# Transposing k and q of batches 2 to 7 on TensorE instead of by DMA

## The chip, the cores and the metric

The kernel runs on one core of a Trainium2 chip. The metric is the time of one execution in microseconds, as the device counts it. TensorE (PE in the profile), VectorE (DVE), ScalarE (ACT), GpSimd (POOL) and the sync engine (SP, which here only issues DMAs) each work through a list of instructions of their own, in order, and wait for each other by semaphores.

## The reference, cut to what matters

```python
def sm_attn(qq, kk, vv):
    s = scale * np.matmul(qq, kk.transpose(0, 1, 3, 2))
    a = np.exp(s - np.max(s, axis=-1, keepdims=True))
    return np.matmul(a / (np.sum(a, axis=-1, keepdims=True) + 1e-09), vv)

p_packed = sm_attn(p, k, v)              # 8 batches, 8 heads, 32 packed rows of 64
attn = sm_attn(q, p_packed, p_packed)    # 576 rows a head
x = attn.transpose(0, 2, 1, 3).reshape(4608, 512)
h = x @ w_in                             # 512 x 2048
g = h * (1.0 / (1.0 + np.exp(-beta * h)))
out = g @ w_out                          # 2048 x 512
```

## The kernel before

The work goes batch by batch, eight batches of 576 rows. For one batch `b`, in the names that the lists of the kernel use:

- `ld`, `cast`: k, v and q are loaded in float32 by DMAs of SP (L446, L454; L461 for batches 0 and 1) and cast to bfloat16, for batches 2 to 7 on GpSimd (L481, L487).
- `tr`, `trr`, `T`, `rk`, `rq`: k and q are transposed, so that the 64 elements of a head lie on partitions. For batches 0 and 1 (`PE_BATCHES = 2`) TensorE does it (L399): one `tr` is eight 128x128 transposes into one PSUM bank, `trr` the last two; an evacuation of each bank follows on VectorE or ScalarE (`T`, L547 and L549, of 128x1024; `rk` and `rq`, L570 and L572, of 128x256). For batches 2 to 7 one DMA transpose each does it (L559), from SBUF to SBUF, issued by SP.
- `s1`, `e1`, `z1`, `pun`, `pp`: the first attention (scores, exponent, sums, product with v, pack).
- `s2`, `e2`, `z2`, `l2`, `n2`, `A2`: the scores of the second attention, their exponents, and these divided by their sums.
- `w`, `W`: the packed values are multiplied with `w_in` first, so that the second attention and the first layer become one product.
- `h`, `g` (`hr`, `gr` for the last 64 rows): that product, 16 pieces of 128x512, and silu on ScalarE (L944).
- `o` and `take` (`add` for batch 0): the product with `w_out` and its evacuation. In batches 1 to 7 the first 512 rows go by Strassen's scheme: seven products `p`/`P` per batch, with the sums `S` of g on VectorE (L1150), sums of `w_out` once (`T4`, L1124), and the reads `R` of the banks (L1180, L1182).
- `store`: DMAs to the output, issued by SP.

PSUM has eight banks here: 2 for `h`, 2 for `o`, and 4 for everything of attention (`att`), transposes and `w` included.

The order in which each engine does these tasks is written out in `SEQUENCE`, one list for each engine. `Planner.run` walks the lists and emits the instructions in that order. With its own table of costs it also places *fillers*: 128x128 matmuls on a tile of ones (`keep_warm`, into a bank of `o`), where it expects TensorE to be idle in the first 60 us (`WARM_UNTIL`). They are real instructions and take their time, whether TensorE would have been idle or not.

Of the kernel before, what the change touches and what calls it, by code (L numbers as in the profile page):

```python
# [8 lines left out]
B, H, S, D = 8, 8, 576, 64  # L9
# [6 lines left out]
bf16 = mybir.dt.bfloat16  # L16
# [9 lines left out]
TS = 9  # L26
# [17 lines left out]
LAG = 0.4  # L44
# [4 lines left out]
def TILED(key):  # L49
# [14 lines left out]
        ("p0_tr",), ("tr", 0, "k", 0), ("bcol",), ("tr", 0, "k", 1), ("brow", 0), ("trr", 0, "k"), ("s1r", 0),  # L64
        ("s1", 0, 0), ("s1", 0, 1), ("tr", 0, "q", 0), ("brow", 1), ("z1", 0), ("tr", 0, "q", 1), ("trr", 0, "q"),
        ("pun", 0, 0), ("pun", 0), ("tr", 1, "k", 0), ("s2", 0, 0), ("z2", 0, 0), ("tr", 1, "k", 1), ("trr", 1, "k"),
        ("z2", 0, 1), ("brow", 2), ("s2", 0, 1), ("w", 0, 0), ("s1r", 1), ("s1", 1, 1), ("s1", 1, 0), ("z2", 0, 2),
        ("h", 0, 1), ("h", 0, 0), ("w", 0, 1), ("h", 0, 2), ("tr", 1, "q", 0), ("z1", 1), ("h", 0, 3), ("h", 0, 7),
        ("pun", 1, 0), ("h", 0, 4), ("h", 0, 6), ("pun", 1), ("tr", 1, "q", 1), ("h", 0, 5), ("brow", 3),
        ("o", 0, 2, 1), ("o", 0, 3, 1), ("o", 0, 3, 3), ("s2", 1, 0), ("o", 0, 2, 3), ("o", 0, 3, 5), ("o", 0, 2, 5),  # L70
        ("z2", 1, 0), ("o", 0, 2, 7), ("z2", 1, 1), ("o", 0, 3, 7), ("w", 0, 2), ("o", 0, 0, 1), ("o", 0, 0, 3),
        ("o", 0, 0, 5), ("w", 1, 0), ("o", 0, 1, 1), ("o", 0, 1, 3), ("h", 0, 8), ("h", 0, 11), ("w", 0, 3),
        ("w", 1, 1), ("h", 0, 10), ("o", 0, 1, 5), ("o", 0, 0, 7), ("h", 0, 9), ("h", 0, 14), ("w", 1, 2),
        ("h", 0, 13), ("h", 0, 15), ("o", 0, 1, 7), ("trr", 1, "q"), ("p_tr", 0), ("h", 0, 12), ("h", 1, 6),
        ("o", 0, 0, 9), ("h", 1, 1), ("h", 1, 4), ("w", 1, 3), ("o", 0, 1, 9), ("h", 1, 11), ("h", 1, 2), ("p_tr", 1),
        ("o", 0, 0, 11), ("h", 1, 8), ("h", 1, 0), ("o", 0, 0, 13), ("o", 0, 1, 11), ("h", 1, 9), ("o", 0, 0, 15),
        ("h", 1, 12), ("o", 0, 1, 13), ("h", 1, 10), ("o", 0, 1, 15), ("o", 0, 3, 9), ("s2", 1, 1), ("o", 0, 3, 11),
        ("s1r", 2), ("s1", 2, 0), ("o", 0, 3, 13), ("o", 0, 3, 15), ("s1", 2, 1), ("o", 0, 2, 9), ("o", 0, 2, 11),
        ("h", 1, 3), ("o", 0, 2, 13), ("o", 0, 2, 15), ("h", 1, 14), ("z1", 2), ("h", 1, 5), ("p", 1, 1, 0),
        ("z2", 1, 2), ("h", 1, 13), ("h", 1, 7), ("p", 1, 1, 1), ("pun", 2, 0), ("h", 1, 15), ("p", 1, 1, 2),  # L80
        ("pun", 2), ("P", 1, 1), ("p", 1, 2, 0), ("p", 1, 2, 1), ("p", 1, 2, 2), ("s2", 2, 0), ("s2", 2, 1),
        ("hr", 0, 0), ("P", 1, 2), ("hr", 0, 1), ("z2", 2, 0), ("p", 1, 6, 0), ("p", 1, 6, 1), ("p", 1, 6, 2),
        ("P", 1, 6), ("w", 2, 0), ("p", 1, 5, 0), ("p", 1, 5, 1), ("p", 1, 5, 2), ("p", 1, 7, 0), ("s1r", 3),
        ("P", 1, 5), ("s1", 3, 1), ("p", 1, 7, 1), ("z2", 2, 1), ("p", 1, 7, 2), ("P", 1, 7), ("p", 1, 3, 0),
        ("p", 1, 3, 1), ("z2", 2, 2), ("s1", 3, 0), ("hr", 1, 0), ("p", 1, 4, 0), ("p", 1, 4, 1), ("w", 2, 2),
        ("p", 1, 4, 2), ("h", 2, 6), ("P", 1, 4), ("h", 2, 1), ("p", 1, 3, 2), ("h", 2, 2), ("z1", 3), ("h", 2, 8),
        ("o", 1, 4, 1), ("h", 2, 9), ("P", 1, 3), ("h", 2, 11), ("pun", 3, 0), ("pun", 3), ("hr", 1, 1),
        ("o", 1, 4, 3), ("h", 2, 3), ("w", 3, 0), ("h", 2, 12), ("h", 2, 13), ("o", 1, 4, 5), ("o", 1, 4, 7),
        ("h", 2, 7), ("h", 2, 15), ("o", 1, 4, 9), ("o", 1, 4, 11), ("h", 2, 0), ("w", 3, 2), ("h", 2, 14),
        ("h", 2, 4), ("o", 1, 4, 13), ("p", 2, 1, 0), ("h", 2, 5), ("h", 2, 10), ("o", 1, 4, 15), ("p", 2, 1, 1),  # L90
        ("p", 2, 1, 2), ("s2", 3, 0), ("s2", 3, 1), ("P", 2, 1), ("p", 2, 2, 0), ("p", 2, 2, 1), ("p", 2, 2, 2),
        ("z2", 3, 0), ("P", 2, 2), ("z2", 3, 1), ("p", 2, 6, 0), ("p", 2, 6, 1), ("p", 2, 6, 2), ("z2", 3, 2),
        ("P", 2, 6), ("s1r", 4), ("s1", 4, 0), ("p", 2, 5, 0), ("s1", 4, 1), ("p", 2, 5, 1), ("p", 2, 5, 2),
        ("P", 2, 5), ("h", 3, 8), ("z1", 4), ("hr", 2, 0), ("p", 2, 7, 0), ("p", 2, 7, 1), ("h", 3, 12), ("h", 3, 13),
        ("pun", 4, 0), ("pun", 4), ("hr", 2, 1), ("p", 2, 7, 2), ("h", 3, 10), ("P", 2, 7), ("h", 3, 9), ("w", 4, 0),
        ("h", 3, 3), ("h", 3, 1), ("p", 2, 3, 0), ("p", 2, 3, 1), ("h", 3, 2), ("h", 3, 15), ("p", 2, 4, 0),
        ("p", 2, 4, 1), ("h", 3, 11), ("h", 3, 5), ("p", 2, 3, 2), ("p", 2, 4, 2), ("h", 3, 6), ("w", 4, 2),
        ("h", 3, 7), ("h", 3, 0), ("P", 2, 4), ("P", 2, 3), ("h", 3, 4), ("h", 3, 14), ("p", 3, 1, 0), ("p", 3, 1, 1),
        ("p", 3, 1, 2), ("P", 3, 1), ("s2", 4, 0), ("s2", 4, 1), ("p", 3, 2, 0), ("p", 3, 2, 1), ("p", 3, 2, 2),
        ("z2", 4, 0), ("P", 3, 2), ("z2", 4, 1), ("p", 3, 6, 0), ("p", 3, 6, 1), ("p", 3, 6, 2), ("P", 3, 6),  # L100
        ("s1r", 5), ("s1", 5, 1), ("z2", 4, 2), ("s1", 5, 0), ("p", 3, 5, 0), ("p", 3, 5, 1), ("p", 3, 5, 2),
        ("P", 3, 5), ("hr", 3, 0), ("p", 3, 7, 0), ("h", 4, 6), ("p", 3, 7, 1), ("p", 3, 7, 2), ("z1", 5),
        ("h", 4, 13), ("hr", 3, 1), ("P", 3, 7), ("p", 3, 3, 0), ("h", 4, 12), ("h", 4, 1), ("pun", 5, 0), ("pun", 5),
        ("p", 3, 3, 1), ("h", 4, 14), ("h", 4, 15), ("w", 5, 0), ("h", 4, 4), ("p", 3, 4, 0), ("h", 4, 2),
        ("p", 3, 3, 2), ("h", 4, 8), ("p", 3, 4, 1), ("h", 4, 9), ("p", 3, 4, 2), ("h", 4, 0), ("w", 5, 2),
        ("h", 4, 7), ("h", 4, 3), ("P", 3, 4), ("P", 3, 3), ("h", 4, 10), ("h", 4, 5), ("o", 3, 4, 1), ("o", 3, 4, 3),
        ("h", 4, 11), ("p", 4, 1, 0), ("p", 4, 1, 1), ("p", 4, 1, 2), ("s2", 5, 0), ("s2", 5, 1), ("P", 4, 1),
        ("o", 3, 4, 5), ("o", 3, 4, 7), ("z2", 5, 0), ("o", 3, 4, 9), ("o", 3, 4, 11), ("z2", 5, 1), ("z2", 5, 2),
        ("o", 3, 4, 13), ("hr", 4, 0), ("o", 3, 4, 15), ("hr", 4, 1), ("p", 4, 6, 0), ("p", 4, 6, 1), ("p", 4, 6, 2),
        ("p", 4, 2, 0), ("p", 4, 2, 1), ("P", 4, 6), ("h", 5, 1), ("h", 5, 15), ("p", 4, 2, 2), ("s1r", 6),  # L110
        ("s1", 6, 1), ("h", 5, 3), ("h", 5, 10), ("P", 4, 2), ("p", 4, 7, 0), ("s1", 6, 0), ("h", 5, 7),
        ("p", 4, 7, 1), ("p", 4, 5, 0), ("p", 4, 5, 1), ("p", 4, 5, 2), ("P", 4, 5), ("h", 5, 13), ("p", 4, 7, 2),
        ("P", 4, 7), ("z1", 6), ("pun", 6, 0), ("pun", 6), ("h", 5, 4), ("h", 5, 8), ("p", 4, 4, 0), ("p", 4, 4, 1),
        ("h", 5, 6), ("h", 5, 9), ("w", 6, 0), ("h", 5, 11), ("p", 4, 4, 2), ("h", 5, 0), ("P", 4, 4), ("h", 5, 14),
        ("p", 4, 3, 0), ("h", 5, 5), ("p", 4, 3, 1), ("h", 5, 2), ("p", 4, 3, 2), ("h", 5, 12), ("P", 4, 3),
        ("p", 5, 1, 0), ("p", 5, 1, 1), ("p", 5, 1, 2), ("s2", 6, 0), ("s2", 6, 1), ("P", 5, 1), ("p", 5, 2, 0),
        ("p", 5, 2, 1), ("p", 5, 2, 2), ("P", 5, 2), ("p", 5, 6, 0), ("z2", 6, 0), ("z2", 6, 1), ("p", 5, 6, 1),
        ("p", 5, 6, 2), ("P", 5, 6), ("s1r", 7), ("s1", 7, 0), ("z2", 6, 2), ("s1", 7, 1), ("p", 5, 5, 0),
        ("p", 5, 5, 1), ("p", 5, 5, 2), ("hr", 5, 0), ("p", 5, 7, 0), ("P", 5, 5), ("p", 5, 7, 1), ("p", 5, 7, 2),
        ("P", 5, 7), ("w", 6, 2), ("h", 6, 0), ("h", 6, 5), ("p", 5, 3, 0), ("p", 5, 3, 1), ("hr", 5, 1),  # L120
        ("h", 6, 10), ("p", 5, 3, 2), ("p", 5, 4, 0), ("h", 6, 3), ("p", 5, 4, 1), ("h", 6, 9), ("p", 5, 4, 2),
        ("h", 6, 4), ("P", 5, 3), ("h", 6, 15), ("z1", 7), ("h", 6, 1), ("P", 5, 4), ("h", 6, 2), ("pun", 7, 0),
        ("h", 6, 14), ("o", 5, 4, 1), ("pun", 7), ("h", 6, 13), ("o", 5, 4, 3), ("o", 5, 4, 5), ("h", 6, 8),
# [239 lines left out]
class Kernel:  # L363
# [160 lines left out]
    def readers(self, b, x):  # L524

        if b < 0:
            return []
        return [("pun", b)] if x == "v" else [("tr", b, x, 0), ("tr", b, x, 1)] + [("trr", b, x)] * (b < PE_BATCHES)
# [966 lines left out]
```

## Time and profile before

| What | Value |
|---|---|
| time, median of 3 runs | 241.2 us (240.27 to 241.45) |
| the profiled execution | 240.81 us, of which 239.0 us are the span that the profile shows |
| TensorE | 231.6 us busy (97%), 2598 matmuls, granted clock 1.0 throughout |
| weight loads of TensorE | 158.0 us (66%), beside the matmuls |
| VectorE, ScalarE, GpSimd | 155.4 us (65%), 179.3 us (75%), 62.4 us (26%) |
| the DMA queue of SP | its packets took 82.1% of 16 engines' span, 53.62 MB |
| fillers | 196 matmuls on ones |
| DMA transposes | 6 of k, 6 of q |

The busy share of TensorE counts each matmul from start to end, and matmuls overlap: a 128x512 matmul of `h` lasts 380 ns, but the chain of waits shows four of them in a row as 0.86 us, one every 215 ns. So the time that a matmul costs its engine is read from the distance of two starts, and a full bar may hide small gaps.

### The profile page before, as it was taken

What the parts mean: (1) busy time and instruction counts of PE and PEld (TensorE: products, weight loads), DVE (VectorE), ACT (ScalarE), POOL (GpSimd) and SP (SyncE); (2) the same over time, 40 slices, a digit from 0 to 9 for tenths busy, and PEclk for the clock granted to TensorE, in tenths of its full rate; (3) what the DMA queues carried; (4) which work ended last, traced back from release to release, by engine and by line L of the source; (5) the groups of instructions that cost most, each with busy time, mean ns of one, the idle gap of its engine ahead of it and who ended that gap; (6) DMA issues with size and microseconds to landing.
All of it is one profiled execution on the core that took longest, in us unless ns stands there. A gap on an engine that the chain in (4) does not pass through costs nothing.

```text
span 239.0 us, 6151 instructions
## 1 busy us (share of the span) xinstructions
PE 231.6 (97%) x2598; PEld 158.0 (66%) x2598; DVE 155.4 (65%) x249; ACT 179.3 (75%) x318; POOL 62.4 (26%) x75
## 2 busy tenths in 40 slices
PE   7999999999979999999999999999999999999994
PEld 7777643444567754786588656785786647668893
DVE  2646878899669947877495555656668167814731
ACT  4758889889769875996699678796886769768410
POOL 3051305333430660573032604080016000000000
PEclk9999999999999999999999999999999999999999
DMA  6999999999999999998999999949695632003033
GB/s 222 394 387 388 410 367 347 280 313 235 270 215 276 287 229 214 333 272 150 181 306 310 198 272 209 297 100 223 165 319 166 148 129 48 0 0 151 27 132 90
DMA packets 67267, 54.14 MB, mean 227 GB/s; under 512 B 38980, under 2 KB 58820, under 8 KB 66728
## 3 DMA queue, kind: packets, MB, share of 16 engines
q1 hardware_dynamic: 67072, 53.62, 82.1%
q8 instruction: 20, 0.33, 0.6%
q10 hardware_dynamic: 168, 0.14, 0.2%
q14 instruction: 7, 0.06, 0.1%
HBM read 37.23 MB, written 9.44 MB: 195 GB/s over the span
## 4 chain that ended last, share of the span: by engine, by line
PE 74%; DMA 16%; DVE 3%; SPq 3%; issue 1%; POOL 1%; ACT 1%; POOLq 0%
PE o_ps L394 42%; PE h_ps L394 19%; DMA w_out<-in_moe_w_out_dram 9%; DMA qT<-q_bf 3%; PE hr_ps L394 3%; PE w_ps L394 3%; DMA v<-in_v_dram 3%; PE s_ps L394 2%; SPq L559 2%; PE z_ps L394 2%; DMA p<-in_p_dram 2%; PE pp_ps L394 1%; DVE w_out_bf L1413 1%; SPq L461 1%; PE brow_ps L394 1%
## 5 line engine op out<-in xcount | busy, mean ns | idle before, releaser
L944 ACT ACTIVATE g_main<-h_ps 128x512 bf16<-128x512 f32 x128 | 72.3, 596 | 30.0 <-PE h_ps L394 29.4
L394 PEld LDWEIGHTS <-g_main 128*128 128x128 bf16 x624 | 59.0, 98 | 25.6 <-issue 3.2
L394 PE MATMUL h_ps<-A2T,W_bf 128*128 128x512 bf16 x256 | 70.6, 380 | 0.2
L394 PE MATMUL o_ps<-w_out_bf,g_main 128*128 128x256 bf16 (+1 forms) x400 | 61.2, 290 | 0.0
L909 DVE SCALAR_TENSOR_TENSOR W_bf<-w_ps,rz,beta_bc 128x512 bf16<-128x512 f32 x64 | 44.6, 744 | 16.3 <-PE w_ps L394 16.1
L394 PEld LDWEIGHTS <-W_bf 128*128 128x128 bf16 x512 | 32.0, 98 | 19.4 <-issue 5.2
L409 ACT ACT_TABLE_LOAD x24 | 30.8, 1283 | 1.1 <-PEq L1479 0.7
L394 PE MATMUL o_ps<-w_sum,g_main 128*128 128x256 bf16 x224 | 31.0, 273 | 0.0
L481 POOL CAST v_bf<-v 128x1024 bf16<-128x1024 f32 x12 | 14.0, 1182 | 58.9 <-DMA v<-in_v_dram 58.9
L1180 DVE TENSOR_TENSOR o_sb<-o_ps,o_sb 128x512 f32<-128x512 f32 x21 | 14.4, 688 | 21.1 <-PE o_ps L394 14.9
L394 PE MATMUL o_ps<-w_sum,g_sum 128*128 128x256 bf16 x224 | 28.1, 273 | 0.0
L394 PEld LDWEIGHTS <-g_sum 128*128 128x128 bf16 x224 | 21.2, 98 | 3.9 <-issue 0.8
L481 POOL CAST q_bf<-q 128x1024 bf16<-128x1024 f32 x12 | 13.2, 1122 | 21.4 <-DMA q<-in_q_dram 15.9
L394 PE MATMUL o_ps<-ones 128*128 128x128 bf16 x196 | 16.0, 238 | 1.1 <-DVE ones L1245 1.1
L394 PE MATMUL o_ps<-w_out_bf,g_rem 128*128 128x512 bf16 (+1 forms) x80 | 16.8, 337 | 0.0
L394 PEld LDWEIGHTS <-ones 128*128 128x128 bf16 x196 | 13.5, 108 | 3.7 <-issue 2.0
L1182 DVE COPY o_sb<-o_ps 128x512 f32<-128x512 f32 x13 | 8.9, 688 | 8.7 <-PE o_ps L394 8.7
L481 POOL CAST k_bf<-k 128x1024 bf16<-128x1024 f32 x12 | 12.4, 1040 | 8.5 <-DMA k<-in_k_dram 4.8
L850 DVE TENSOR_TENSOR A2T<-E2T,rz 128x512 bf16<-128x512 bf16 x16 | 12.2, 782 | 3.3 <-ACT rz L845 3.3
L964 ACT ACTIVATE g_rem<-hr_ps 128x512 bf16<-128x512 f32 x16 | 9.3, 597 | 4.6 <-PE hr_ps L394 4.5
L809 ACT ACTIVATE E2T<-s_ps,rz 128x512 bf16<-128x512 f32 x16 | 10.5, 686 | 2.7 <-PE s2r_ps L394 2.2
L394 PEld LDWEIGHTS <-g_rem 128*128 128x128 bf16 x80 | 7.6, 98 | 5.0
(114 smaller groups left out, 267.1 us busy)
## 6 DMA issues: line engine op xcount, KB each, us to landing
k<-in_k_dram SPq DMA_DIRECT2D x6, 1024.0 KB, 10.2
q<-in_q_dram SPq DMA_DIRECT2D x6, 1024.0 KB, 9.7
v<-in_v_dram SPq DMA_DIRECT2D x6, 1024.0 KB, 6.4
out_dram<-o_sb SPq DMA_DIRECT2D x10, 512.0 KB, 3.1
w_in<-in_moe_w_in_dram SPq DMA_DIRECT2D x4, 1024.0 KB, 10.7
w_out<-in_moe_w_out_dram SPq DMA_DIRECT2D x4, 1024.0 KB, 11.3
out_dram<-o_sb SPq DMA_DIRECT2D x12, 256.0 KB, 4.3
k<-in_k_dram SPq DMA_DIRECT2D x4, 576.0 KB, 6.3
```

The lines of the kernel that those rows point to most:

```text
L394: return self.nc.tensor.matmul(out, lhsT, rhs, start=start, stop=stop, tile_position=pos, skip_group_check=True)
L409: self.nc.scalar.preload_act_table_set(SETS[mode])
L461: nc.sync.dma_start(t[:].rearrange("p (i e f) -> p i e f", i=2, e=2)[:, i], src[b].rearrange("(e i a) (s t) d -> i (a s) e (t d)", e=2, i= ...
L481: self.copy[engine](o[:, 0:2048].rearrange("p (t h d) -> p h t d", t=4, h=8)[:, h], t[:, 0:2048].rearrange("p (h t d) -> p h t d", h=8, t= ...
L559: nc.sync.dma_start_transpose(t[:], st[b, x][:])
L809: nc.scalar.activation(st[b, "E2"][:, i, 0:SM], st[b, "s2", i][:], AF.Exp, scale=st[b, "rz1"][:, 2 + i : 3 + i])
L850: nc.vector.tensor_tensor(part(st[b, "A2"], i), part(st[b, "E2"], i), st[b, "rz2"][:, i] if i < 2 else st[b, "rz2r"][:], ALU.mult)
L909: nc.vector.scalar_tensor_tensor(st[b, "W"][:, r, cols].rearrange("q (f p) -> q f p", f=4), st[b, "w", m][:].rearrange("q (p f) -> q f p", ...
L944: nc.scalar.activation(st[b, "g"][:, ft, :], st[b, "h", ft][:], AF.Silu)
L964: nc.scalar.activation(st[b // 2, "gr"][:, 8 * half : 8 * half + 8, o : o + 64], st[b, "hr", half][:].rearrange("p (f n) -> p f n", f=8), ...
L1180: nc.vector.tensor_tensor(o, x, o, ALU.add)
L1182: self.copy[engine](o, x)
```

## The change

- The DMA transposes and their cost entry (`LAG`) go. The tasks `tr`, `trr`, `T`, `rk` and `rq`, which were there for batches 0 and 1, now exist for all batches: for each of the 12 tensors (k and q of batches 2 to 7) 18 transposes on TensorE into three `att` banks and three evacuations, which go to VectorE or ScalarE as the lists say. They keep the layout that the DMA transpose had.
- For batches 2 to 7 each `tr` waits for both main casts, and `trr` for the cast of the rest.
- `SEQUENCE` is a new one for all engines, with the new tasks in it. The multiset of all other tasks is the same, but the order differs everywhere, and some tasks moved between VectorE, ScalarE and GpSimd.

The code, without the lists:

```diff
         def transpose(x, i):
             st[b, x, "ps", i] = ps = self.att(f"{x}T_ps", bf16)
             for t in range(8):
-                a = 128 * (TS * i + t)
+                a = 128 * ((TS if b < PE_BATCHES else 8) * i + t)
                 self.tp(ps[:, 128 * t : 128 * t + 128], st[b, x][:, a : a + 128], self.identr[:])
...
-            if x == "k":
+            if x == "k" or b >= PE_BATCHES:
...
-        def transpose_dma(x):
-            st[b, x, "T"] = t = self.tr.tile([128, 18, 128], bf16, tag=f"{x}T", name=f"{x}T")
-            nc.sync.dma_start_transpose(t[:], st[b, x][:])
-
...
-                a = 128 * (TS * u + 8)
+                a = 128 * (TS * u + 8 if b < PE_BATCHES else 16 + u)
...
-            if x == "q":
+            if x == "q" and b < PE_BATCHES:
...
         for x in "kq":
-            if b >= PE_BATCHES:
-                d = self.task(
-                    ("tr", b, x, 0), "SP", 2.7, lambda x=x: transpose_dma(x),
...
-                continue
             for i in range(2):
                 tr = self.task(
                     ("tr", b, x, i), "PE", (0.45, 0.15), lambda x=x, i=i: transpose(x, i),
-                    [("cast", b, x, i)] + old, rank, takes="att",
+                    [("cast", b, x, j) for j in (range(2) if b >= PE_BATCHES else (i,))] + old, rank, takes="att",
                 )
```

A piece of the new lists, around batches 2 and 3 (TensorE's, and VectorE's up to the first Strassen sum):

```python
"PE":  ... ("h", 1, 6), ("h", 1, 4), ("tr", 2, "k", 1), ("tr", 2, "k", 0), ("h", 1, 1), ("h", 1, 8), ...
       ("trr", 2, "k"), ("s2", 1, 1), ... ("s1r", 2), ("s1", 2, 0), ... ("tr", 2, "q", 0), ("tr", 2, "q", 1),
       ("o", 0, 3, 9), ("o", 0, 3, 11), ("z1", 2), ("tr", 3, "k", 1), ("tr", 3, "k", 0), ("h", 1, 14), ...
"DVE": ... ("rq", 1), ("T", 2, "k", 0), ("T", 2, "k", 1), ("W", 1, 6), ("add", 0, 0), ("rk", 2), ("W", 1, 7),
       ("T4", 1), ("T4", 2), ("add", 0, 1), ("T", 2, "q", 0), ("T4", 3), ("T4", 4), ("T", 3, "k", 0),
       ("add", 0, 2), ("T", 2, "q", 1), ("i1", 2), ("T", 3, "k", 1), ("add", 0, 3), ("S", 1, 1), ...
```

Counted over the built instructions: TensorE gets 216 transposes more and has 185 fillers instead of 196; VectorE has 28 `T` instead of 6 and 9 `rk`/`rq` instead of 2, ScalarE 4 `T` instead of 2 and 7 `rk`/`rq` instead of 2; ScalarE loads its function tables 22 times instead of 24; SP issues 12 DMAs less.

## The prediction

> **What bounds the kernel now.** I read the page's busy lines and slices first, then TensorE's busy time by windows, then who made TensorE wait, and only then the chain that ended last.
>
> ```profile
> PE 231.6 (97%) x2598; PEld 158.0 (66%) x2598; DVE 155.4 (65%) x249; ACT 179.3 (75%) x318; POOL 62.4 (26%) x75
> PE   7999999999979999999999999999999999999994
> DVE  2646878899669947877495555656668167814731
> PEclk9999999999999999999999999999999999999999
> DMA  6999999999999999998999999949695632003033
> ```
>
> The share of 97% alone would prove little, as it is a mean and counts overlapping matmuls. The slices say more: TensorE is full from the second slice to the last but one, with one dent (slice 12, about 66 to 72 us), at full clock. The DMA engines are as full up to 180 us, and there it is the question who waits for them. The windows (columns: window, its length, busy time and instructions, clock, DMA share, GB/s):
>
> ```profile
> 50.00:60.00 10.00, 10.00 (x77) 1.00 1.13 251
> 60.00:70.00 10.00, 8.10 (x101) 1.00 1.12 250
> 70.00:220.00 150.00, 150.00 (x1646) 1.00 0.80 198
> ```
>
> and TensorE's waits from 60 us on:
>
> ```profile
> PE pp_ps L394 <- POOL v_bf L487: 1.0, 1, 1.0
> PE s_ps L394 <- DMA qT<-q_bf: 0.8, 1, 0.8
> ```
>
> From 30 us on TensorE has two visible holes, 1.0 us for the cast of v and 0.8 us for the transposed q of batch 2: 1.8 us in all. After 70 us it never waits. Against this stands the chain:
>
> ```profile
> 50.20 4.71 SPq L559
> 54.96 6.06 DMA v<-in_v_dram
> 61.02 8.15 DMA qT<-q_bf
> 69.75 0.57 PE hr_ps L394 x16
> ```
>
> It follows the last releaser, so it runs through the DMA transposes between 50 and 70 us although TensorE was working beside them all but 1.8 us. Those DMAs were only just late; their 12.9 us were not TensorE's loss. So the kernel is bound by TensorE's stream from about 30 us on. Before that the loads set the pace, and fillers stand in TensorE's idle time.
>
> **What is added to TensorE.** The old transposes of batches 0 and 1 show the price. From the timeline (start, length, and the form):
>
> ```profile
> 16.85 0.62 PE L399 MATMUL kT_ps<-identr,k_bf 128*128 128x128 bf16 x8
> 17.31 0.22 PE L394 MATMUL o_ps<-ones 128*128 128x128 bf16 x1
> ...
> 19.80 0.27 PE L399 MATMUL krT_ps<-identr,k_bf 128*128 128x128 bf16 x2
> 19.91 0.38 PE L394 MATMUL z_ps<-E2T,bones 128*128 128x512 bf16 x1
> ```
>
> Eight transposes delay the next matmul by 17.31 - 16.85 = 0.46 us, two by 0.11 us, though one alone is shown with 220 ns. One tensor needs 2 x 0.46 + 0.11 = 1.03 us, twelve need 12.3 us. Nothing hides this, since the engine that does it is the bound, and all 216 stand after the first `h` in the list, where TensorE is full.
>
> [...]
>
> **What is taken from TensorE.** The fillers go from 196 to 185. In the row that starts at 18.01 us, 20 of them delay the next matmul (19.14) by 1.13 us, 57 ns each: 11 save 0.6 us. The remaining 185 are in the stream whatever happens, so the head does not get shorter by more than that without TensorE waiting less than it did.
>
> **What is removed from the DMA side.** Twelve transposes of SP:
>
> ```profile
> L559 SPq DMA_TRANSPOSE kT<-k_bf x6: 2718/4303/6232, 50.2 to 164.0; - x6
> L559 SPq DMA_TRANSPOSE qT<-q_bf x6: 2730/3196/4708, 61.0 to 185.4; - x6
> ```
>
> Each holds SP's queue 3 to 4 us (minimum, median, maximum in ns), and they wait there for casts (16.7 us for q_bf); loads and stores behind them start sooner. Of this TensorE can gain the 0.8 us hole (no DMA for qT any more) and the 1.0 us hole (v of batch 2 was loaded behind a transpose, and TensorE asks for it 3 us later now). I take both: -1.8 us. Bounds: 0 if another wait takes their place, -1.8 visible, and about 1.5 us more, because busy matmuls overlap by some 160 ns (380 shown against 215 from start to start) and gaps shorter than this hide in a full bar.
>
> **What moves on the other engines.** VectorE gets 22 `T` of 0.69 us and 7 of `rk`/`rq` of 0.29 us, and gives or takes a few copies: +17 us, to about 172 of 250 us. ScalarE gets 2 `T` of 1.01 us and 5 of 0.37 us, but loads two tables less (2 x 1.28 us): about +3 us. Over the whole run both have room; it is tight from 40 to 60 us, where VectorE was already busy for 18.75 of 20 us. Before the first Strassen sum the new VectorE list has six `T` and one `rk` more: 6 x 0.69 + 0.29 = 4.4 us. TensorE has 6 x 0.46 + 0.11 = 2.9 us more in the same stretch, so that VectorE's own need grows by 1.5 us against it, and VectorE then idled for 3.5 us (busy 6.47 of 10 us from 60 to 70 us), nearly all of it a wait for `pp_ps`; this slack is the cover. I count nothing, and 4.4 us at the high end if it is gone.
>
> New waits of TensorE: each `tr` waits for GpSimd's casts, each `s1r`, `s1` and `s2` for the evacuations, and 36 more tiles pass through the four `att` banks. Behind a waiting `tr` stands everything, since the list is strict. The tightest place is `tr` of k of batch 2, behind the sixth `h` or so of batch 1: before, GpSimd finished that cast at 50.2 us, and TensorE will be there near 50 us by its list. That is a wait between 0 and 1 us. The load of k is now one transfer earlier in SP's list (the load of p moved ahead), so I take 0. Elsewhere evacuations have microseconds: between `trr` of k for batch 2 and its `s1r` stand five products of 0.43 us.
>
> **The sum.** Profiled execution 240.8 us, which is 0.4 us below the median of 241.2, within the spread of its runs (240.27 to 241.45). 240.8 + 12.3 - 0.6 - 1.8 = 250.7 us. The end is unchanged: 3.6 us from the last matmul to the end of the span in both, as the last tasks are the same.
>
> **Rivals.**
>
> The chain taken at its word: the main part begins earlier because k and q of batch 2 no longer pass through the DMA queue. Place: 50 to 70 us. Price: 4.71 + 8.15 = 12.9 us less. Then 240.8 + 12.3 - 0.6 - 12.9 = 239.6 us, faster by 0.7%. It decides from the point where TensorE has some 12 us of idle time or fillers there to be given back. For it: the chain's own shares (16% DMA). Against it: the windows, with 1.8 us of idle time from 50 to 70 us and no fillers there. Chance 0.03, of which I leave a part to an unnamed better order of the head.
>
> VectorE becomes late: the 4.4 us of evacuations in the stretch before the first Strassen sum delay `W`, `add` and the sums, and TensorE waits for these. 250.7 + 4.4 = 255.1 us. For it: the slices of VectorE. Against it: its 3.5 us of slack right behind. Chance 0.15.
>
> The transposes cost what a single one shows (220 ns): 216 x 0.22 = 47.5 us instead of 12.3, 285.9 us. Against it: the starts above. Chance 0.01. That most of the gain and cost cancel, within 0.5% of 241.2, needs both holes and 9 us more of hidden gaps; chance 0.02.
>
> The forecast itself has 0.79. Range: downward 250.7 - 1.5 (hidden gaps) - 1.7 (TensorE was busy for 8.28 us of the first 10; another order of the head could win the rest) = 247.5; upward 255.0, VectorE's rival almost whole. What remains outside is under 2 in 10. Half a per cent, 1.2 us, is about what a measurement of this kernel can tell from no change: faster by more 0.03, within it 0.02, slower by more 0.95.
>
> **What would show it.** Right: TensorE's windows after 70 us still full, 288 transposes of k and q on the rows of `tp` with starts about 57 ns apart, 185 fillers, no DMA_TRANSPOSE, the DMA share well under 1 after 60 us, VectorE near 172 us, span near 249 us, no wait of TensorE over 1 us after 60 us. Wrong: TensorE waits for `kT` or `qT` evacuations or for `k_bf`; the first Strassen products start before 63 us (they start at 62.2 us now, and have 2.9 us of transposes ahead of them in the new list); or transposes that start more than 100 ns apart.

## The result and the profile after

The changed kernel takes 253.12 us (median of 4 runs, 250.94 to 254.87), the kernel before 240.75 us on the same chip (4 runs, 240.27 to 241.45): 1.0481 times the time before [1.0403, 1.0559; here and below the brackets are the 95% interval of the ratio]. The ratio leaves out the slow execution of 254.87 us, so it is lower than 253.12 to 240.75. The prediction was 250.7 us, 247.5 to 255.0.

The busy lines and slices of the changed kernel, as before:

```profile
PE 243.1 (96%) x2774; PEld 171.7 (68%) x2803; DVE 172.2 (68%) x270; ACT 183.3 (72%) x333; POOL 59.1 (23%) x73
PE   6997999999999999999999999999999999999993
DVE  2558797998979787958688638726677287822621
PEclk9996799999999999999999999999999999999999
DMA  7999989999598970592189404990030002300315
```

TensorE is as full as it was, and the dent at 66 to 72 us is gone. The DMA engines have room from 63 us on and are idle for whole slices from 95 us on. VectorE has the 172 us that were predicted. New is the dent in the fourth slice of TensorE, and in the granted clock there and behind it. The windows of TensorE (window, its length, busy time and instructions, clock, DMA share, GB/s):

```profile
20.00:22.00 2.00, 0.59 (x13) 0.75 1.02 379
22.00:24.00 2.00, 2.00 (x25) 0.50 1.08 432
24.00:26.00 2.00, 2.00 (x21) 0.50 1.01 419
26.00:28.00 2.00, 2.00 (x25) 0.54 0.98 398
28.00:30.00 2.00, 2.00 (x30) 1.00 1.04 390
...
60.00:70.00 10.00, 9.95 (x97) 1.00 0.81 179
70.00:220.00 150.00, 148.95 (x1746) 1.00 0.50 149
```

The clock is half from 21.0 to 27.8 us. Around the start of this, TensorE waits, and its waits of over half a microsecond from 10 us on are these two:

```profile
PE w_ps L403 <- DVE w_in_bf L1398: 1.4, 1, 1.4
...
PE s2r_ps L403 <- DVE qT L575: 0.6, 1, 0.6
```

VectorE's timeline tells why `w_in_bf` is late (start, length, form, and what ended the idle time before it):

```profile
19.55 0.69 DVE L1321 CAST p_dup<-p 96x1024 bf16<-96x1024 f32 x1 [0.85 <-DMA p<-in_p_dram]
20.16 1.53 DVE L1398 CAST w_in_bf<-w_in 128x1024 bf16<-128x1024 f32 x1
```

VectorE's list has `p_dup` of half 0 ahead of the second cast of `w_in`. It stood 0.85 us for the load of p. This load is now issued at 5.31 us and lands 14.22 us after that, and half of the copy has moved to VectorE (before: issued at 35.7 us, both halves on GpSimd from 44.2 us on, with no cast of `w_in` behind them). Then came `p_dup`, and the cast of `w_in` took 1.53 us where the casts of its form just before and after it took 0.69 and 0.68, beside a `p_dup` on GpSimd (19.65 to 21.14 us). The first `w` needs this cast.

Not every execution is hit in this way. The eight executions of the changed kernel that were timed (four above, four of the repetition further down), each with its mean granted clock:

| Time, us | 250.94 | 251.10 | 252.83 | 253.13 | 253.25 | 253.29 | 253.42 | 254.87 |
|---|---|---|---|---|---|---|---|---|
| Clock | .999 | .998 | .993 | .990 | .990 | .991 | .990 | .987 |

The time follows the clock: two executions at .998 and above take 251.0 us, six below take 1.8 to 3.9 us more. The profile shown above is of the slowest. In this stretch the 36 fillers from 22.81 us on delay the next matmul by 3.98 us, 111 ns each; in the profile of the execution of 251.10 us, at a clock of 1.0, the same 36 delay it by 2.10 us, 58 ns each. Of the 6.8 us at half clock TensorE was idle for the first 0.7, so that at most 3.1 us of matmuls, an estimate from these numbers, are lost to the clock; the first Strassen product starts at 69.19 us, against 65.53 in the profile of the execution of 251.10 us. These 3.7 us are nearly the whole distance of the two. No profile fell on the other five slower executions: that their clock fell in the same place is concluded from their mean clock and from the next two experiments.

### The profile page after: what moved, and what is told of

It reads as the page before. It is cut to its first block, busy times and chain, and to the rows that moved or that the text cites. A ratio compares the mean times of both kernels' runs of the same rounds, so it can differ in the third digit from the quotient of the medians.

```text
span 253.0 us, 6549 instructions
## 1 busy us (share of the span) xinstructions
PE 243.1 (96%) x2774; PEld 171.7 (68%) x2803; DVE 172.2 (68%) x270; ACT 183.3 (72%) x333; POOL 59.1 (23%) x73
## 4 chain that ended last, share of the span: by engine, by line
PE 79%; DMA 8%; DVE 6%; SPq 3%; issue 1%; ACT 0%
PE o_ps L403 44%; PE h_ps L403 18%; DMA p<-in_p_dram 7%; PE w_ps L403 4%; PE hr_ps L403 3%; PE qT_ps L408 3%; PE kT_ps L408 2%; SPq L463 2%; DVE W_bf L905 2%; PE s_ps L403 2%; PE z_ps L403 2%; DVE w_out_bf L1409 2%; PE pp_ps L403 1%; DMA q<-in_q_dram 1%; SPq L1184 1%
## 5 line engine op out<-in xcount | busy, mean ns | idle before, releaser
L403 PE MATMUL h_ps<-A2T,W_bf 128*128 128x512 bf16 x232 | 66.8, 379 | 0.4
L403 PE MATMUL o_ps<-w_sum,g_sum 128*128 128x256 bf16 x224 | 28.9, 273 | 0.1
L490 POOL CAST v_bf<-v 128x1024 bf16<-128x1024 f32 x12 | 13.3, 1107 | 28.2 <-PE pp_ps L403 26.7
L403 PE MATMUL o_ps<-ones 128*128 128x128 bf16 x185 | 16.9, 255 | 1.1 <-DVE ones L1241 1.1
L403 PEld LDWEIGHTS <-ones 128*128 128x128 bf16 x185 | 14.7, 118 | 4.3 <-issue 1.9
L1178 ACT COPY o_sb<-o_ps 128x512 f32<-128x512 f32 x16 | 9.3, 583 | 6.5 <-PE o_ps L403 6.5
L846 DVE TENSOR_TENSOR A2T<-E2T,rz 128x512 bf16<-128x512 bf16 x16 | 12.4, 790 | 0.9 <-ACT rz L841 0.9
L556 DVE COPY kT<-kT_ps 128x1024 bf16<-128x1024 bf16 x16 | 10.9, 687 | 3.0 <-PE kT_ps L408 2.9
L408 PEld LDWEIGHTS <-k_bf 128*128 128x128 bf16 x144 | 9.3, 98 | 4.5 <-ACT k_bf L502 1.9
```

What stands on the lines that cost most here:

```text
L403: return self.nc.tensor.matmul(out, lhsT, rhs, start=start, stop=stop, tile_position=pos, skip_group_check=True)
L408: return self.nc.tensor.matmul(out, in_, ident, is_transpose=True, skip_group_check=True)
L490: self.copy[engine](o[:, 0:2048].rearrange("p (t h d) -> p h t d", t=4, h=8)[:, h], t[:, 0:2048].rearrange("p (h t d) -> p h t d", h=8, t= ...
L556: self.copy[engine](st[b, x, "T"][:, 8 * i : 8 * i + 8], ps.rearrange("p (t n) -> p t n", t=8))
L846: nc.vector.tensor_tensor(part(st[b, "A2"], i), part(st[b, "E2"], i), st[b, "rz2"][:, i] if i < 2 else st[b, "rz2r"][:], ALU.mult)
L1178: self.copy[engine](o, x)
```

## The experiments

Three things had to be told apart: what the wait and the half clock cost, whether the transposes alone make the other 10 us as the sum said, and whether the new order of the lists has a price or a gain of its own. The expectations call it theory A that the wait for `w_in_bf` lowers the clock and makes the spread, C that VectorE comes late, E that the new order costs time by itself, and G that the head of the kernel hides its transposes.

### The cast of w_in first

```diff
 "DVE":
-    ("p_dup", 0), ("w_in", 0, 0), ("beta", 3), ...
+    ("w_in", 0, 0), ("p_dup", 0), ("beta", 3), ...
```

> The changed kernel with one swap in VectorE's list: the cast of w_in (0, 0) ahead of the first copy p_dup, which waits for the load of p (the planner then places 182 fillers instead of 185). Theory A (head of line: VectorE's wait for p holds back w_in, so w, so TensorE idles 1.4 us, and after that idle time the granted clock halves for several us): the hole before w is gone, no half clock after 20 us, span 249 us or less, time 250 to 251 us in every run instead of 250.9 to 254.9. Rival B (the half clock has nothing to do with this wait): some runs still show half clock and 252 to 255 us. Rival C (the extra time over 250.7 is VectorE's evacuations between 40 and 65 us): time stays at 252 to 255 us whatever the clock does in the head.

251.13 us (250.96 to 251.58), 1.0422 [1.0393, 1.0451]. The wait is gone: this is the first `w` in TensorE's timeline, which in the changed kernel began at 21.75 us, behind 1.41 us of idle time.

```profile
20.16 0.41 PE L403 MATMUL w_ps<-w_in_bf,pp 64*32 64x512 bf16 x8
```

With it the spread is gone: four executions within 0.6 us, at a clock of .997 or more. Of 253.12 us, 2.0 are thus owed to the wait and the half clock that goes with it. But the kernel is no faster than the undisturbed executions of the changed kernel, 250.94 and 251.10 us. The idle time by itself cost nothing that can be seen, and TensorE's timeline shows why: at 32 us, TensorE in the kernel with the swap waits for an evacuation of k of batch 1. This row of it

```profile
32.30 0.25 PE L403 MATMUL s1r_ps<-pT,kT 128*64 128x64 bf16 x4 [0.91 <-DVE kT L577]
```

starts at 32.31 us, without a wait, in the profiled execution of 251.10 us: up to there VectorE's list sets the pace, and an earlier `w` gains nothing.

### Fillers in the place of the wait

```diff
+                if t.key == ("w", 0, 0):
+                    for _ in range(26):
+                        self.filler()
```

> The changed kernel with 26 more fillers (1.5 us at 57 ns) straight ahead of the first w, in the place where TensorE waited 1.4 us; the order of all lists as in the changed kernel. Theory A, in its part on the clock (idle time is what halves the clock): no half clock after 20 us, and since the fillers take the place of idle time, 250.5 to 251.5 us. Rival B (something else halves the clock): the half clock is still there in some runs, and these take 253 to 255 us.

251.92 us (251.56 to 252.25), 1.0452 [1.0421, 1.0482], with a clock of .996 or more. The fillers hold the clock as well as the order does; the mean of .996 is of the profiled execution, whose windows show a clock of 1.00 up to 220 us. The time is 0.8 us above the first experiment and above what was expected. The fillers did not delay the `w`, which starts at 21.47 us, against 21.51 in the undisturbed execution. The profiled execution is 0.5 us slower than that one, and this it has lost before the first Strassen product (65.98 us instead of 65.53), with a wait of 0.3 us for `A2T` on VectorE; whether the fillers bring this about isn't shown.

### The changed kernel once more, and one with a hole but fewer fillers

The changed kernel was run again, unaltered, for the table above:

> The changed kernel once more, unaltered. If the half clock is what spreads its times: every run obeys 250.8 us plus the time that its clock lost, so a run with a clock of 0.999 to 1.000 takes 250.6 to 251.1 us, and one with 0.987 takes 254 to 255 us; a profile at full clock has its first Strassen product at 65 to 66 us, not at 69.2 us. If the wait for p itself is the cost, this product stays at 67 us or later at full clock, and the time at 252 us or more.

253.19 us (251.10 to 253.29), 1.0494 [1.0446, 1.0542]. This time the profile fell on the execution of 251.10 us. It has the same wait, 1.17 us instead of 1.41, and the clock stays at 1.0 through the head:

```profile
21.51 0.41 PE L403 MATMUL w_ps<-w_in_bf,pp 64*32 64x512 bf16 x8 [1.17 <-DVE w_in_bf L1398]
```

So nearly the same hole does or does not go with a half clock. Time and clock are where the clock theory expected them, and so is the first Strassen product, at 65.53 us.

In the other kernel, on top of the first experiment, the 36 fillers ahead of the second `w` are left out:

```diff
-                fill(at)
+                if t.key != ("w", 0, 1):
+                    fill(at)
```

> The changed kernel with the swap of p_dup, less the 36 fillers between the first two w, so that TensorE is idle there for some 2 us at 21 us; nothing else differs. Theory A (idle time around 20 us is what halved the clock): half clock for several us from about 21 to 25 us on, in most runs, and up to 3.5 us more, 251.5 to 254.5 us. Rival B (idle time there does not matter): 250.5 to 251.5 us at full clock.

250.89 us (250.77 to 251.48), 1.0444 [1.0420, 1.0468]. TensorE waits for 1.59 us:

```profile
22.26 0.74 PE L404 MATMUL w_ps<-w_in_bf,pp 64*32 64x512 bf16 x8 [1.59 <-DVE w_in_bf L1399]
```

In the profiled execution the clock stays at 1.0 nevertheless; in the three others its mean is .990, and yet these take 250.8 to 251.5 us, less than theory A expected. So such a hole goes with a lowered clock in some executions and not in others. Why the lowered clock cost nothing here isn't shown, as no profile fell on those three; it would fit with a head in which TensorE, relieved of some 2 us of fillers, is not what is waited for. The 2 us themselves gained 0.2: the wait of 0.9 us at 32 us is there in this kernel too.

### Each transpose of batches 2 to 7 twice

On top of the first experiment; `trr` in the same way:

```diff
-            for t in range(8):
+            for t in [*range(8), *(range(8) if b >= PE_BATCHES else ())]:
```

> On top of the swap of the first kernel, each of the 216 transposes of batches 2 to 7 is made twice into the same place. Theory A (TensorE's stream is the bound and a transpose costs it 57 ns): 12.3 us more than with the swap alone, 262 to 264 us. Rival C (VectorE or another engine is the bound in part of the run): clearly less than 12 us more. Rival D (a transpose costs its engine more than 57 ns among other work): over 14 us more.

263.57 us (263.45 to 263.60), 1.0934 [1.0906, 1.0963]. That is 12.4 us over the first experiment for 216 transposes more, 57 to 58 ns each, the price that the prediction read off the starts. 3.2 us of it came before the first Strassen product and 9.3 us after it. Hardly any of this second dose was hidden.

### Each evacuation twice

On top of the first experiment, the copy of each `T` of batches 2 to 7 is issued twice:

```diff
-                self.copy[engine](st[b, x, "T"][:, 8 * i : 8 * i + 8], ...)
+                for _ in range(2 if b >= PE_BATCHES else 1):
+                    self.copy[engine](st[b, x, "T"][:, 8 * i : 8 * i + 8], ...)
```

> On top of the swap of the first kernel, each of the 24 evacuations T of 128x1024 of batches 2 to 7 is made twice (22 on VectorE, 0.69 us each, 2 on ScalarE, 1.01 us each: 17 us more). Theory A (VectorE has slack nearly everywhere): 0 to 3 us more than with the swap alone. Rival C (VectorE is late between 40 and 65 us or later): 4 us more for the six evacuations before the first Strassen sum alone, up to 17 us in all.

255.50 us (254.82 to 255.96), 1.0597 [1.0557, 1.0636]: 4.4 us over the first experiment for some 17 us more of copies. In the windows from 40 to 60 and 60 to 80 us (here and below: busy time of PE, PEld, DVE, ACT and POOL in this order, then clock, DMA share and GB/s) VectorE is nearly full:

```profile
40.00:60.00 20.00, 19.27 (x168) 9.44 (x171) 19.11 (x31) 17.23 (x32) 10.55 (x10) 1.00 1.06 315
60.00:80.00 20.00, 18.82 (x236) 14.52 (x236) 19.58 (x25) 15.46 (x32) 14.51 (x12) 1.00 0.84 227
```

The rival "VectorE becomes late" is therefore real but needs a second dose; three quarters of the added work were still hidden.

### The new order without the transposes

The code of before with the lists of the first experiment for TensorE, VectorE and ScalarE, out of which the transposes and evacuations of batches 2 to 7 are struck. SP and GpSimd have the new order up to the loads and casts of batch 1, with the early load of p, and from batch 2 on the old one, with the 12 DMA transposes:

```diff
 "PE":
-    ("h", 1, 4), ("tr", 2, "k", 1), ("tr", 2, "k", 0), ("h", 1, 1), ...
+    ("h", 1, 4), ("h", 1, 1), ...
 "SP":
+    ("tr", 2, "k", 0), ... ("tr", 2, "q", 0), ... ("tr", 7, "q", 0),
```

> The new lists without the new work: the kernel before with the lists of TensorE, VectorE and ScalarE of the changed kernel (with the swap of p_dup), from which all transposes and evacuations of batches 2 to 7 are struck, the 12 DMA transposes back, and the loads, stores and casts of batches 2 to 7 in the old order on SP and GpSimd. Theory A (all of the loss is TensorE time of the transposes; the lists themselves are worth about as much as the old ones): 12.3 us less than the changed kernel with the swap, and up to 2 us back where DMA transposes are late: 239 to 241 us. Rival E (the new order itself costs part of the 10 us): 242 to 248 us.

243.61 us (243.28 to 243.88), 1.0140 [1.0114, 1.0166]. Theory A expected the time before, and the kernel is about 3 us slower, as rival E had it. Where, the first of the Strassen products tells, which mark the end of the head; in TensorE's timeline of the kernel before, then of this one:

```profile
62.20 0.60 PE L394 MATMUL o_ps<-w_out_bf,g_main 128*128 128x256 bf16 x4
```

```profile
65.22 0.60 PE L212 MATMUL o_ps<-w_out_bf,g_main 128*128 128x256 bf16 x4
```

The new order reaches this point 3.0 us later without a single transpose of batches 2 to 7. From there to the last matmul it needs 172.1 us, the kernel before 173.2. TensorE is not full in this head (windows as above):

```profile
20.00:40.00 20.00, 18.88 (x269) 12.16 (x266) 16.47 (x31) 16.31 (x32) 5.88 (x5) 1.00 1.04 399
40.00:60.00 20.00, 19.13 (x157) 8.47 (x156) 17.47 (x27) 17.77 (x34) 7.29 (x9) 1.00 1.07 303
```

and its waits from 25 to 70 us are for silu on ScalarE and for an evacuation on VectorE:

```profile
PE h_ps L212 <- ACT g_main L762: 2.3, 2, 1.5
PE s1r_ps L212 <- DVE kT L390: 0.9, 1, 0.9
```

### One transpose of each bank

The lists here are wholly those of the first experiment, but of each bank only the first transpose is made:

```diff
-            for t in range(8):
+            for t in range(8 if b < PE_BATCHES else 1):
...
-            for u in range(2):
+            for u in range(2 if b < PE_BATCHES else 1):
```

> The changed kernel with the swap of p_dup, in which of the transposes of batches 2 to 7 only the first of each bank is made: 36 instead of 216. The evacuations read that one block over and over, so they, all waits and all lists stay; the k and q that the scores then use are not the transposed ones. It leaves out 180 transposes. Theory A (each costs TensorE 57 ns, wherever it stands): 180 x 57 ns = 10.3 us less than the swap alone, 240.5 to 241.2 us. Theory G (some of them, those before the first Strassen product, stand in time that is open in the new order, so that leaving them out saves less): 242 to 244 us.

243.57 us (243.41 to 244.35), 1.0135 [1.0103, 1.0167], 7.6 us less than the first experiment for 180 transposes less, which at 57 ns are 10.3 us. Before the first Strassen product 43 are left out, 2.4 us; it starts at 65.21 us instead of 65.51. After it 137 are left out, 7.8 us, and 7.1 us are gained. So transposes after the head cost nearly their 57 ns (52 here), and those in the head almost nothing, as the order is not ready earlier without them. The opposite dose above showed that this room is used up: there, 2.9 us more in the head cost 3.2 us.

### Parts of the change alone

Three kernels, the first and the third on the lists of before. In the first, loads and transposes are only reordered, so that both holes of TensorE (1.0 and 0.8 us) would go:

```diff
 "SP":
-    ("ld", 3, "k", 0), ("ld", 2, "v", 2), ("ld", 3, "k", 2), ("tr", 2, "q", 0),
+    ("ld", 2, "v", 2), ("tr", 2, "q", 0), ("ld", 3, "k", 0), ("ld", 3, "k", 2),
 "POOL":
-    ("cast", 3, "k", 0), ("cast", 2, "v", 2),
+    ("cast", 2, "v", 2), ("cast", 3, "k", 0),
```

> The kernel before, with its DMA transposes, and two places moved: SP loads all of v of batch 2 and issues the transpose of its q ahead of the load of k of batch 3, and GpSimd casts the rest of v of batch 2 ahead of k of batch 3. Theory A (TensorE's only holes after 30 us, 1.0 and 0.8 us, are there because these come late): both holes gone, 1.0 to 1.8 us less than before, 239.0 to 240.0 us. Rival F (the transpose of k of batch 3 or the loads of batch 3 become late instead): no gain or a loss of up to 2 us.

246.18 us (245.33 to 247.26), 1.0238 [1.0207, 1.0270], slower instead of a little faster. The two holes are gone (TensorE is busy for 10.00 us from 60 to 70 us), but k of batch 3 is now late, and the clock falls during that wait (first TensorE's waits, then its windows):

```profile
PE s1r_ps L212 <- DMA kT<-k_bf: 4.3, 1, 4.3
```

```profile
74.00:76.00 2.00, 0.00 (x0) 1.00 0.74 138
76.00:78.00 2.00, 0.00 (x0) 0.89 1.09 175
78.00:80.00 2.00, 1.85 (x16) 0.50 0.89 283
80.00:82.00 2.00, 2.00 (x15) 0.76 1.08 353
```

In this order, what the DMA queue gave to v and q of batch 2 it took from k of batch 3; other orders of these transfers weren't tried.

The second moves k and q of batch 2 and k of batch 3 to TensorE, on the lists of the order experiment:

```diff
+ON_PE = ((2, "k"), (2, "q"), (3, "k"))
...
-            if b >= PE_BATCHES:
+            if b >= PE_BATCHES and (b, x) not in ON_PE:
```

> The new lists with a part of the new work: the kernel with the new lists and DMA transposes (243.6 us), but k and q of batch 2 and k of batch 3 are transposed on TensorE, which are those that the new list places before or just behind the first Strassen product; the other nine by DMA. Theory G (in the new order TensorE waits for ScalarE's silu from 50 to 65 us, and these transposes stand in time that is open anyway): 242.5 to 244.2 us. Theory A as predicted (every transpose costs its 57 ns, 1.03 us a tensor, wherever it stands): 246 to 247 us.

250.77 us (250.43 to 251.68), 1.0409 [1.0363, 1.0455]. Neither theory expected this. `tr` waits for casts that the old order of GpSimd makes late:

```profile
PE kT_ps L217 <- POOL k_bf L299: 3.3, 2, 2.0
```

and the clock is half from 64.7 to 71.5 us. It says nothing on the head's price, only that the lists of SP and GpSimd belong to those of TensorE.

The third moves one tensor alone, q of batch 2, which is the one that TensorE waited for:

```diff
 "PE":
     ("z1", 2),
+    ("tr", 2, "q", 0),
     ("h", 1, 5), ("p", 1, 1, 0),
+    ("tr", 2, "q", 1),
     ...
     ("p", 1, 1, 1),
+    ("trr", 2, "q"),
 "DVE":
     ("i1", 2),
+    ("T", 2, "q", 0), ("T", 2, "q", 1), ("rq", 2),
 "SP":
-    ("tr", 2, "q", 0),
```

> The kernel before with one of the twelve tensors moved: q of batch 2 is transposed on TensorE between z1 of batch 2 and the first Strassen products, its three evacuations follow i1 of batch 2 on VectorE, where that was idle, and SP has one DMA transpose less; all else in the old order. Theory A (TensorE gains the two holes of 1.0 and 0.8 us, since the transposes stand in the first and the second was the DMA itself, and pays 1.03 us): 0.7 us less than before, 239.6 to 240.6 us. Rival F (the DMA queue from 50 to 75 us is what TensorE's list hangs on, so one transfer less moves more than the holes, and one thing late moves it the other way): 1.5 us or more in either direction.

239.93 us (12 runs, 239.15 to 240.96) against 240.54 us (17 runs, 239.78 to 242.75): 0.9966 [0.9944, 0.9989]. It beats both kernels, by 0.6 us over the one before: a small gain, but the interval leaves out 1. It was expected (0.7 us). 1.03 us of transposes went into 1.8 us of holes; no wait of TensorE is left after 60 us, and its windows are now:

```profile
60.00:70.00 10.00, 9.87 (x144) 1.00 0.82 218
70.00:220.00 150.00, 150.00 (x1629) 1.00 0.80 199
```

## Why the prediction held, and where it did not

**The sum.** The undisturbed execution of the changed kernel takes 251.1 us, 10.3 over the profiled one before; the sum said 9.9. The signs that it named for this are there: a span of 249.3 us, full windows after 70 us, no wait of TensorE over 1 us after 60 us. One of its signs of being wrong is there too: TensorE waits 0.6 us for an evacuation of `qT` at 18.8 us, and 0.2 us (1.1 in the first profile) for `k_bf` at 6 us; but these are of batch 0, and no wait for the new tasks of batches 2 to 7 is shown there. Split by three marks of TensorE's timeline (us):

| | before | after, undisturbed | difference |
|---|---|---|---|
| to the first Strassen product | 62.20 | 65.53 | +3.3 |
| from there to the last matmul's end | 173.24 | 180.00 | +6.8 |
| from there to the end of the span | 3.58 | 3.79 | +0.2 |

After the mark stand 166 of the transposes: 9.5 us at 57 ns, less 1.8 us of holes, makes 7.7, of which 6.8 are found; where the other 0.9 went isn't shown. The mechanism is shown by dose there: 7.1 us less when 7.8 are taken out, 9.3 more when 9.5 are put in.

**The price of a transpose.** 57 ns, read from the starts. TensorE's timeline of the changed kernel shows a `tr` of batch 4 amid other work:

```profile
91.82 0.61 PE L408 MATMUL kT_ps<-identr,k_bf 128*128 128x128 bf16 x8
92.26 0.59 PE L403 MATMUL o_ps<-w_out_bf,g_rem 128*128 128x512 bf16 x2
```

Eight delay the next matmul by 0.44 us. The doubling confirms it in the measured time: 12.4 us for 216.

**"Nothing hides this": wrong in the head.** TensorE was full in the head of before (busy for 20.00 us from 20 to 40 us and for 19.89 us from 40 to 60 us), and the prediction took it to be the bound there in the new lists too. In the new order it is not: that head ends 3.0 us later than before even without the transposes, and with them only 0.3 us later still. Leaving out 43 transposes, or 36 fillers, moved its end by no more than 0.3 us. The 2.9 us of the sum stand in the head by accident: the order's own 3.0 us took the place of the transposes' 2.9. The prediction's sign of being wrong, first Strassen products before 63 us, looked for a gain only. That 250.7 lies 0.4 us from the undisturbed time is thus in part luck. Which part of the order costs the 3.0 us wasn't separated; without the transposes ScalarE's silu is waited for longest, and this stays open.

**"That is a wait between 0 and 1 us", taken as 0: the wrong wait.** It was looked for at `tr` of k of batch 2; it came at `w` at 20 us. The prediction noted that the load of p moves ahead, but counted this only as something that brings k forward. The one step that it didn't make is to look who waits for p at the head of an engine's list: `p_dup` on VectorE, with the cast of `w_in` behind it. The wait cost nothing by itself, but with the half clock that goes with it 2 us at the median, and 3.9 in the profiled execution. This term, absent from the sum, is 2.0 of the 2.4 us from 250.7 to 253.1.

**VectorE.** No cost was the right value: 172.2 us as predicted (169.5 in the undisturbed execution), and a quarter of a second dose is felt (4.4 of 17 us).

**The chain at its word.** It fell as argued: the DMA transposes are gone, and the 12.9 us of the chain did not come. What there was to gain, the 1.8 us, is what the one-tensor kernel bought.

## What to carry to other kernels

On TensorE, which is the bound here behind the head, a moved transpose cost about its distance from start to start (52 to 58 ns by the doses above, 57 from the starts); the move paid only for the one tensor of twelve that filled holes which its move removed (0.6 us less). Before work is moved onto a strict list, look at what each early transfer's first consumer has behind it: a copy that waits at the head of its engine's list can hold up work that has nothing to do with it (here `p_dup` stood 0.85 us for p, and TensorE 1.41 us for the cast of `w_in` behind it). And when the order of a whole kernel changes, price the order apart from the operations, with the operations taken out; a total that agrees can be a sum of two errors.

## What the runs showed of the hardware

- In the profiled execution of the changed kernel, gaps of TensorE of 0.57 us (to 18.76) and 1.41 us (20.34 to 21.75) went with 6.83 us of half clock, from 21.02 us on, so the granted clock fell 0.7 us into the second gap; 4.3 us of waiting in the reordered kernel went with about 3.4 us of it, an estimate from the windows. With the second gap filled, or removed by the order, all eight executions kept a mean clock of .996 or more. But the changed kernel with 1.17 us in the same place kept a clock of 1.0 there once, and the one with fewer fillers did with 1.59, so what decides it stays open.
- A VectorE copy of 128x1024 from float32 to bfloat16 took 1.53 us in both profiles of the changed kernel, where the same form just before it took 0.69; in the first of the two it ran beside the GpSimd `p_dup` of 1.49 us (19.65 to 21.14 us). With the cast moved ahead of `p_dup`, it took 0.69.
